# Where the key and query transposes and the sums stand among the slots of an attention stage on TensorE

## The chip, the cores and the metric

The kernel runs on one core of a Trainium2 chip. The metric is the device time of one execution in microseconds (us). PE is TensorE, the matrix engine; PEld is its loading of weights; DVE, ACT and POOL are the vector, scalar and general engines; SP issues most of the DMAs.

## What is computed

Attention over 8 batches, 12 heads, 448 tokens and a head size of 64, with normalized queries and keys, and then a mixture of experts over the 3584 tokens, each of which goes to one of 8 experts:

```python
q_n, k_n = rmsnorm(q, g_q), rmsnorm(k, g_k)
scores = (1 / sqrt(64)) * q_n @ k_n.transpose(0, 1, 3, 2)
attn = softmax(scores)                       # over the keys
x = (attn @ v) -> [3584, 768]                # tokens x (heads * 64)
logits = x @ w_gate + modality_bias[modality_id]
e = argmax(logits);  gate = softmax(logits)[e]
out = gate * (relu(x @ w1[e]) @ w2[e])       # for each token its expert
```

## The kernel before

The first half of the time is attention, the second the experts. The change touches attention alone.

A **unit** is two heads of one batch, so there are 48 units (`NU`). A unit has seven **slots** (`NJ`), one for each group of 128 rows out of its 2 x 448 = 896. Attention is a loop over slots `n`; slot `n` belongs to unit `i` and has the place `j` in it (`i, j = divmod(n, NJ)`, so `j` runs from 0 to 6). In each slot PE computes, in this order:

- `st` (L851): the scores of the current unit, keys by queries, two matmuls (four in place 3) into one buffer of the two-buffer PSUM pool `ps_s`. ACT takes the exponential of it into `p`.
- `sa` (L823, in place 3 L818): scores of a unit two ahead, only to find the maxima; DVE reduces them.
- then whatever else the slot has.

The other work of PE is spread over the slots by a table of numbers, `PLAN`. For a unit `u` an entry such as `'tk': 21` puts the work into slot `7u - 21`; others count from a later unit. The works, with their line on PE:

- `tr` (L752): four transposes of normalized keys (`tk`) or queries (`tq`), 112 rows each, into one buffer of the two-buffer PSUM pool `ps_t`. Four readers empty it, in this order: `a0`, the first copy on ACT (`xw<-tr`), whose result goes on by two DMAs on SP; the difference on DVE between the transposes and that copy (`xw<-tr,xw`), with two more DMAs; then two copies of half the rows on ACT, `a1` and `a2` (`w1w<-tr`). ACT's `a1` waits for DVE's difference.
- `mt` (L834): one transpose of the unit's maxima, also from `ps_t`. ACT copies it (`xw<-mt`) and a DMA takes it to the place where the scores read it.
- `av` (L890): value products, attention times values, in four parts `c` of two matmuls. They stand in places 1, 1, 4 and 6 (`'av': (1, 1, 4, 6)`).
- `sums` (L905): the sums of the exponentials, once for two units, in place 2 (`'sm': 2`); `gates` (L912): the gate logits, once for four units, in place 6.
- `recips` (`sp`, L924): transposes of sums and gate logits, once for four units, from `ps_t`; in place 2 (`'rc': 9`). DVE reads them.
- `xt` (L947): transposes of a unit's output, from `ps_t`, in place 4. DVE reads them.

Five kinds of work so share the two buffers of `ps_t`. A buffer is taken by whoever asks when it is free, and else the one whose last reader is done first.

The other engines' part is laid out by lists: what is put at `pre["A"]` or `pre["V"]` for slot `n` is done on ACT or DVE before that slot's exponential and maxima, what is put at `post` after them:

```python
run(pre["A"], n)
run(pre["V"], n)
pump(...)                 # one operation of the routing, if there is any
if ex:
    ex()                  # exponential of this slot's st, on ACT
for f in sm:
    f()                   # maxima of this slot's sa, on DVE
pump(...)
run(post, n)
```

ACT also squares queries and keys for the norms (`xrw<-r`) and DVE reduces the squares (`at_hlw<-xrw`); POOL multiplies by the norms. Each engine works its list in order, so an instruction that waits holds back all behind it.

Of the kernel before, what the change touches and what calls it, by code (L numbers as in the profile page):

```python
# [30 lines left out]
NT1 = NB1 * S  # L31
BIG = float(1 << 20)
ET = mybir.EngineType
PLAN = {'rtj': 6, 'rushat': 36, 'av': (1, 1, 4, 6), 'xt': 4, 'xte': (2, 5), 'sm': 2, 'la': 6, 'rc': 9, 'csv': (1,), 'csj': (3, 6), 'csd': (1, 1), 'cse': (2, 1), 'sa': 14, 'mt': 6, 'tk': 21, 'tq': 18, 'nq': 26, 'nk': 26, 'sk': 49, 'sq': 50, 'rs': 48, 'ld': 58, 'first': {('sq', 0): -22, ('sk', 0): -22, ('nk', 0): -21, ('nq', 0): -20, ('sq', 1): -21, ('sk', 1): -21, ('sq', 2): -20, ('sk', 2): -20, ('nk', 1): -18, ('nq', 1): -18, ('tk', 0): -18, ('tq', 0): -18, ('sa', 0): -14, ('tk', 1): -13, ('tq', 1): -11, ('sa', 1): -7, ('mt', 0): -6, ('tk', 2): -8, ('tq', 2): -8, ('nq', 2): -14, ('nk', 2): -14, ('nq', 3): -2, ('nk', 3): -1, ('sq', 3): -8, ('sk', 3): -8, ('sq', 4): -9, ('sk', 4): -9, ('sq', 6): -6, ('sk', 6): -4, ('sk', 7): -7, ('sq', 8): 5, ('sk', 8): 5, ('nk', 7): 15, ('nq', 9): 31, ('tq', 3): 4, ('mt', 1): 0, ('nq', 5): 10, ('mt', 8): 50, ('rs', 0): -21, ('rs', 2): -18, ('nq', 8): 35, ('rs', 5): -7, ('mt', 2): 8, ('nq', 7): 18, ('mt', 5): 30, ('sk', 9): 15, ('tk', 9): 43, ('mt', 6): 36, ('nq', 6): 13, ('sa', 5): 22, ('rs', 7): 0, ('rs', 8): 6, ('mt', 4): 22, ('nk', 4): 4, ('ld', 9): 6, ('tk', 5): 15}, 'rs0': {0: 0, 2: 1, 5: 0, 7: 0, 8: 2}, 'sastep': 1, 'start': -22, 'warm': {5: 2, -6: 16, -12: 4, -7: 2, -9: 4, -21: 4}, 'warmn': 2, 'early': 1, 'late0': 1, 'pmp0': 2, 'ramp': 10, 'pmp': (0, 0, 1, 1, 1, 0, 1), 'nv': [(2, 1)], 'pmpa': (1, 0, 1, 0, 1, 1, 1), 'rush': (1, 1, 1), 'ps': [(7, 1)], 'pa': [(6, 0), (6, 1), (5, 1), (5, 0)], 'rtr': 6, 'sml': 4}
MANUAL = {ET.PE, ET.DVE, ET.Activation, ET.Pool, ET.SP}
IOFF = bass.IndirectOffsetOnAxis

# [29 lines left out]
def kernel(  # L67
# [15 lines left out]
    V, A, G = (Deferred(e, n) for e, n in ((nc.vector, "op"), (nc.scalar, "act"), (nc.gpsimd, "dma")))  # L83
# [562 lines left out]
    if True:  # L646
# [33 lines left out]
        def sumsq(u, i):  # L680
# [4 lines left out]
            sq = sq_b[i]  # L685
            if (u, i) in PLAN["pa"]:
                x = T[u][nm].rearrange("p h c d -> p (h c) d")
# [143 lines left out]
        def mt(u):  # L831
            t = T[u]
            ps = ps_t.tile([128, 512], F32, tag="t", name=f"mt{u}")
            PE.transpose(ps[0:NJ, :128], t["mx"], idn)  # L834

            def act():
                ms = ms_b[u % 2]
                A.copy(ms, ps[0:NJ, :128])
                (A if u < 2 else SY).dma_start(t["ql"][64:65].rearrange("p h s -> p (h s)").bitcast(F32),
                            ms.bitcast(F32))  # L840

            return act
# [206 lines left out]
        P = PLAN  # L1049
# [6 lines left out]
        puts, done, routed = [], [], []  # L1056
# [32 lines left out]
        def warm(n):  # L1089
            for _ in range(n):  # L1090
                PE.matmul(wps[:, :128], lhsT=ones, rhs=idn, start=True, stop=True)
# [10 lines left out]
        pre = {e: {} for e in "AV"}  # L1102
        post, fin = {}, {}
        P = PLAN
        CSV, CSJ, CSD, CSE = (P[x] for x in ("csv", "csj", "csd", "cse"))

        def at(where, n, fn):
            where.setdefault(n, []).append(fn)
# [19 lines left out]
        P = PLAN  # L1128
# [39 lines left out]
        for n in range(P["start"], NJ * NU):  # L1168
            i, j = divmod(n, NJ)
            todo = {}  # L1170
            for what, *a in plan.get(n, ()):
                todo.setdefault(what, []).append(tuple(a))
            state["n"] = n
            state["rush"] = i >= P["rushat"]
            warm(P["warm"].get(n, 0))
            ex = st(i, j) if 0 <= i < NU else None
            sm = [sa(*a) for a in todo.get("sa", ())]
            if n < 0:
                warm(P["warmn"])
            for u, c in todo.get("av", ()):  # L1180
                av(u, c)
                if c == 3:
                    at(pre["A"] if j else post, n + (j > 0), lambda u=u: avcopy(u))
            for a in todo.get("sums", ()):
                sums(*a)
            for a in todo.get("gates", ()):
                at(pre["A"], n + 1, gates(*a))
            for a in todo.get("tr", ()):
                a0, a1, a2, d_ = tr(*a)
                if a[0] < P["early"]:  # L1190
                    at(pre["A"], n + 1, a1)
                    at(pre["A"], n + 1, a2)
                    at(pre["A"], n + P["late0"], a0)
                    at(pre["V"], n + P["late0"], d_)
                    continue
                at(pre["A"], n + 1, a0)
                at(pre["V"], n + 1, d_)
                at(post, n + 1, a1)
                at(pre["A"], n + 2, a2)
            for a in todo.get("mt", ()):  # L1200
                at(pre["A"], n + 1, mt(*a))
            for a in todo.get("recips", ()):
                at(pre["V"], n + 1, recips(*a))
                at(pre["V"], n + 1, lambda a=a: done.append(a[0]))
            for a in todo.get("xt", ()):
                at(pre["V"], n + 1, xt(*a))
            if puts and n >= puts[0][0] and n - lastput[0] >= 3:
                lastput[0] = n
                puts.pop(0)[1]()
            if i == NU - 1 and j in XRJ:  # L1210
                at(pre["V"], n + 1, xtr(0, X0, XRJ.index(j)))
            run(pre["A"], n)
            run(pre["V"], n)
            pump(P["rush"][0] if state["rush"] else P["pmpa"][j], j)
            if ex:
                ex()
            for f in sm:
                f()
            pump(P["rush"][1] if state["rush"] else P["pmp"][j], j)
            run(post, n)  # L1220
            for a in todo.get("sq", ()):
                at(pre["V"], n + 1, sumsq(*a))
            for a in todo.get("rs", ()):
                fast.append(("exp", lambda a=a: rstd(*a)))
            pump(P["rush"][2] if state["rush"] else P["pmp0"] if n < P["ramp"] else 0, j)
            if 0 <= i < NU and j in CSJ:
                h = CSJ.index(j)
                more, rest = csum(i, h)
                at(fin, n + CSD[h], more)
                at(fin, n + CSE[h], rest)  # L1230
            run(fin, n)
            for a in todo.get("norm", ()):
                while fast and (a[0] < 9 or a[0] % 3 == 0):
                    pump(1)
                norm(*a, V if a in P["nv"] else G)
                if a[0] == 0 and a[1] == 1:
                    gain_product()
            for a in todo.get("load", ()):
                load(*a)
            if done and len(routed) < B - 1 and done[-1] >= (NP * len(routed) + 5) // 4:  # L1240
                b = len(routed)
                routed.append(b)
                slow.append(("exp", lambda b=b: route(b)))
                slow.append(("pe", lambda b=b: at(pre["V"], state["n"] + 1, route_mm(b))))
                slow.append(("exp", lambda b=b: route_pos(b)))
                if b < B - 2:
                    slow.append(("exp", lambda b=b: put_all(b)))
                if b == NB1 - 1:
                    slow.append(("exp", tables1))
            if n == -4:  # L1250
                load_v(0)
                load_gate()
                SY.dma_start(l_d.rearrange("(p r) w -> p (r w)", p=128), zt)
            for h in range(2):
                if n == NJ * (NU - 5 + h) + 4:
                    wload(0, 0, (h,))
            if n == NJ * (NU - 3) + 4:
                X0 = xload(0)
            if i >= NU - 2 and j < 6:
                split1(i - NU + 2, j, j + 1)  # L1260
            if j < NJ - 1:
                continue
            if i == 0:
                slow += deferred(gate_consts)
            if i == NU - 1:
                for m in sorted(fin):
                    run(fin, m)
                wload(0, 1)
            if (i + 1) % 3 == 0 and 0 < (i + 1) // 3 < 2 * B:
                load_v((i + 1) // 3)  # L1270
# [121 lines left out]
    nv = nc.values_load(state["nsl"], min_val=0, max_val=NS1 + NS2)  # L1392
# [52 lines left out]
```

## Time and profile before

| what | value |
|---|---|
| three timed runs, median (lowest to highest) | 1141.43 us (1140.6 to 1145.1) |
| the profiled execution: time | 1139.65 us |
| the profiled execution: span from first to last instruction | 1137.9 us |
| its granted clock, mean | 0.98 |

The profile is of one execution. A group of its instructions is named by line, engine, operation and out<-in, by the program's names of its buffers: `tr`, `mt`, `sp`, `xt`, `st`, `sa`, `av`, `sm` are the PSUM tiles above. Many works share the line L52 on ACT, DVE and POOL, since a helper records them; they are told apart by their tiles. In the timeline the first column is the start, the second the duration. In a row of windows the busy time of PE, PEld, DVE, ACT and POOL follows, each with its count, then the granted clock of PE (1.00 is full speed), the DMA share and GB/s. In a row of waits stand the total in us, the number of waits and the longest.

### The profile page before, as it was taken

The page shows a single profiled execution, that of the slowest core. Times are in us where ns is not written, and L with a number is a line of the kernel's source. Part 1 is how long each engine was busy: PE and PEld are TensorE (multiplying, and loading weights), DVE is VectorE, ACT ScalarE, POOL GpSimd, SP SyncE. Part 2 cuts the span into 40 slices and gives each one's busy share as a digit, 9 for nine tenths or more (in the row PEclk, how much of TensorE's full clock was granted, in tenths as well). Part 3 has the DMA queues.
Part 4 walks back from the last instruction along what each step waited for, and adds up shares of the span by engine and source line. Part 5 has one row for each costly group of instructions (what it writes and reads, how often), then busy time and mean ns, then how long its engine had stood idle before and what let it go on. Part 6 is the DMA issues. An engine that isn't in the chain of part 4 may idle for free. (4 is left out here: it accounts for less than half of the span.)

```text
span 1137.9 us, 19896 instructions
## 1 busy us (share of the span) xinstructions
PE 1089.8 (96%) x6678; PEld 856.9 (75%) x6678; DVE 863.7 (76%) x1598; ACT 827.7 (73%) x1605; POOL 656.8 (58%) x665
## 2 busy tenths in 40 slices
PE   7899999999999999999999999999999999999993
PEld 6655655566565565555568899999999999999981
DVE  4676778988779988789688987767777677776770
ACT  6878888778787787775666677668776687766770
POOL 4577677777777787777764565444244433345430
PEclk8899999999999999999999999999999999999996
DMA  7656567666576666665725111111161111111360
GB/s 170 169 127 154 127 174 173 167 161 148 141 180 162 163 144 160 168 147 114 212 66 189 26 46 59 40 57 56 43 252 41 56 43 56 32 40 56 115 186 11
DMA packets 101345, 131.78 MB, mean 116 GB/s; under 512 B 29979, under 2 KB 95983, under 8 KB 99696
## 3 DMA queue, kind: packets, MB, share of 16 engines
q1 hardware_dynamic: 83588, 88.57, 32.0%
q0 software_dynamic: 17616, 41.80, 11.7%
q8 instruction: 57, 0.93, 0.4%
q14 instruction: 56, 0.46, 0.1%
q10 hardware_dynamic: 28, 0.01, 0.0%
HBM read 148.74 MB, written 22.38 MB: 150 GB/s over the span
## 5 line engine op out<-in xcount | busy, mean ns | idle before, releaser
L485 PE MATMUL ph<-xw,w1w 128*128 128x256 f32 x2016 | 246.1, 283 | 1.8 <-DVE hlw L52 1.0
L485 PEld LDWEIGHTS ph<-xw,w1w 128*128 128x128 f32 x2016 | 243.9, 192 | 3.8 <-issue 1.4
L52 DVE TENSOR_REDUCE at_hlw<-sa 128x1 f32<-128x448 f32 x336 | 206.9, 618 | 48.3 <-PE sa L823 30.0
L52 DVE TENSOR_TENSOR w1w<-r,w1w 128x256 fp32r<-128x256 f32 x360 | 221.0, 672 | 13.8 <-ACT w1w L52 13.5
L52 ACT CAST w1w<-r 128x256 fp32r<-128x256 f32 x360 | 224.8, 722 | 0.0
L851 PE MATMUL st<-w1w 128*128 128x448 f32 (+1 forms) x480 | 191.7, 448 | 1.1 <-ACT r2w L52 0.8
L851 PEld LDWEIGHTS st<-w1w 128*128 128x128 f32 (+1 forms) x480 | 107.3, 239 | 45.1 <-ACT r2w L52 21.2
L52 ACT ACTIVATE hhw<-ph 128x512 fp32r<-128x512 f32 x56 | 33.5, 598 | 121.8 <-PE ph L485 121.8
L52 POOL TENSOR_TENSOR r2w<-r2w 128x448 f32<-128x448 f32 (+1 forms) x72 | 82.4, 1144 | 68.4 <-DVE r2w L52 30.6
L52 ACT ACTIVATE r2w<-st 128x448 f32<-128x448 f32 x168 | 90.0, 541 | 40.7 <-PE st L851 35.7
L823 PE MATMUL sa<-w1w 128*128 128x448 f32 (+1 forms) x288 | 110.6, 385 | 8.9 <-DVE at_hlw L52 5.8
L515 PE MATMUL py<-w2lw,hhw 128*128 128x384 f32 x448 | 113.9, 335 | 0.0
L851 PE MATMUL st<-w1w,w2ha 65*128 65x448 f32 x288 | 102.5, 376 | 3.1 <-DMA r2w<-in_v_dram 2.5
L52 ACT ACTIVATE at_w2lw<-st 128x448 f32<-128x448 f32 x168 | 89.3, 540 | 13.4 <-PE st L851 11.6
L52 POOL TENSOR_TENSOR xrw<-r,at_hlw 112x512 f32<-112x512 f32 x95 | 97.4, 1045 | 2.5 <-PE tr L752 2.2
L52 POOL DMA_INDIRECT out_dram<-yw,lb_oi x22 | 28.3, 1286 | 122.0 <-ACT yw L52 118.9
L515 PEld LDWEIGHTS py<-w2lw,hhw 128*128 128x128 f32 x448 | 80.9, 188 | 0.0
L52 DVE SCALAR_TENSOR_TENSOR hlw<-ph,hhw 128x512 fp32r<-128x512 f32 x56 | 38.7, 691 | 51.9 <-ACT hhw L52 51.9
L52 ACT ACTIVATE w1w<-tr,gs 64x448 fp32r<-64x448 f32 x96 | 60.3, 629 | 23.0 <-DVE xw L52 22.3
L52 POOL TENSOR_TENSOR r2w<-r2w,at_w2lw 64x448 f32<-64x448 f32 (+1 forms) x48 | 54.9, 1144 | 38.0 <-DVE r2w L52 19.5
L851 PEld LDWEIGHTS st<-w1w,w2ha 65*128 65x128 f32 x288 | 70.9, 246 | 5.4 <-DMA r2w<-in_v_dram 2.7
L52 ACT ACTIVATE xrw<-r 112x512 f32<-112x512 f32 (+1 forms) x124 | 64.6, 526 | 9.7 <-DMA r<-in_k_dram 7.2
(297 smaller groups left out, 2297.9 us busy)
## 6 DMA issues: line engine op xcount, KB each, us to landing
w1w<-xw SPq DMA_DIRECT2D x312, 112.0 KB
r<-in_q_dram SPq DMA_DIRECT2D x48, 224.0 KB
r<-in_k_dram SPq DMA_DIRECT2D x48, 224.0 KB
w2ha<-xw SPq DMA_DIRECT2D x72, 112.0 KB
x_d<-at_w2hb SPq DMA_DIRECT2D x8, 672.0 KB
x_d<-yw SPq DMA_DIRECT2D x8, 672.0 KB
r2w<-in_v_dram SPq DMA_DIRECT2D x16, 288.0 KB
at_w2lw<-in_v_dram SPq DMA_DIRECT2D x16, 288.0 KB
```

The costliest lines, as they stand in the source:

```text
L52: return fn(*a, **kw)
L485: PE.matmul(ps[:, i], lhsT=lt_, rhs=rt_[:, c], start=n == 0, stop=n == 17)
L515: PE.matmul(ps[n][:, :384], lhsT=lt_[:, j, 128 * t : 128 * t + 128], rhs=rt_[:, 384 * n : 384 * n + 384], start=j == 0 and m == 0, stop=j ...
L823: PE.matmul(ps[:, :S], lhsT=t["qq"][r, h, a : a + 128], rhs=t["kk"][h][r], start=True, stop=True)
L851: PE.matmul(ps[:, :S], lhsT=l, rhs=t["qq"][:, h] if first else t["ql"][:, h], start=first and (j != 3 or h == 0), stop=not first and (j != ...
```

## The change

Numbers of the table, and the order within a slot. By the table `sm` goes from 2 to 4, `rc` from 9 to 8, `tk` from 21 to 20, `tq` from 18 to 17 (and one norm, of queries in unit 9, from slot 31 to 32, so that it stays behind what it needs):

```diff
-PLAN = {... 'sm': 2, 'la': 6, 'rc': 9, ... 'tk': 21, 'tq': 18, ...}
+PLAN = {... 'sm': 4, 'la': 6, 'rc': 8, ... 'tk': 20, 'tq': 17, ...}
```

So keys go from place 0 to 1, queries from 3 to 4, sums from 2 to 4 and recips from 2 to 1. Places 1, 4 and 6 hold value products. In the loop the transposes (`tr`, `mt`, `recips`, `xt`) are now issued ahead of the value products, sums and gates, and the readers of `tr` are put at other points of ACT's and DVE's lists:

```diff
+            for a in todo.get("tr", ()):
+                a0, a1, a2, d_ = tr(*a)
+                if a[0] < P["early"]:
+                    at(pre["A"], n + 1, a1)
+                    at(pre["A"], n + 1, a2)
+                    at(pre["A"], n + P["late0"], a0)
+                    at(pre["V"], n + P["late0"], d_)
+                    continue
+                at(post, n, a0)
+                at(post, n, d_)
+                at(pre["A"], n + 1, a1)
+                at(post, n + 1, a2)
+            for a in todo.get("mt", ()):
+                at(pre["A"], n + 1, mt(*a))
+            for a in todo.get("recips", ()):
+                at(pre["V"], n + 1, recips(*a))
+                at(pre["V"], n + 1, lambda a=a: done.append(a[0]))
+            for a in todo.get("xt", ()):
+                at(pre["V"], n + 1, xt(*a))
             for u, c in todo.get("av", ()):
                 av(u, c)
                 if c == 3:
...
                 sums(*a)
             for a in todo.get("gates", ()):
                 at(pre["A"], n + 1, gates(*a))
-            for a in todo.get("tr", ()):
-                a0, a1, a2, d_ = tr(*a)
...
-                at(pre["A"], n + 1, a0)
-                at(pre["V"], n + 1, d_)
-                at(post, n + 1, a1)
-                at(pre["A"], n + 2, a2)
-            for a in todo.get("mt", ()):
-                at(pre["A"], n + 1, mt(*a))
-            for a in todo.get("recips", ()):
-                at(pre["V"], n + 1, recips(*a))
-                at(pre["V"], n + 1, lambda a=a: done.append(a[0]))
-            for a in todo.get("xt", ()):
-                at(pre["V"], n + 1, xt(*a))
```

**PE, places 1 to 3 of unit 10**, a unit in which `recips` stand. Before (the number in a name after the tile is the tile's running number; `tr_1` are keys, `tr_0` queries; the keys' transposes of this unit stand just ahead of the first row, in place 0):

```order
L851 MATMUL st_1_1677<-w1w 128x448
L851 MATMUL st_1_1677<-w1w,w2ha 128x448
L823 MATMUL sa_1_1680<-w1w 128x448
L890 MATMUL av_1682<-at_w2lw 64x448 x4
L834 MATMUL mt_1687<-idn,at_hlw 7x128
L851 MATMUL st_2_1699<-w1w 128x448
L851 MATMUL st_2_1699<-w1w,w2ha 128x448
L823 MATMUL sa_2_1702<-w1w 128x448
L905 MATMUL sm_1704<-at_w2hb,sel 32x448 x2
L905 MATMUL sm_1704<-at_hhw,sel 32x448 x2
L924 MATMUL sp_1709<-idn,at_hlw 112x128 x4
L851 MATMUL st_3_1723<-w1w 128x448 x2
```

and now, in the same places:

```order
L851 MATMUL st_1_1672<-w1w 128x448
L851 MATMUL st_1_1672<-w1w,w2ha 128x448
L823 MATMUL sa_1_1675<-w1w 128x448
L752 MATMUL tr_1_1677<-idn,xrw 128x112 x4
L834 MATMUL mt_1682<-idn,at_hlw 7x128
L924 MATMUL sp_1684<-idn,at_hlw 112x128 x4
L890 MATMUL av_1689<-at_w2lw 64x448 x4
L851 MATMUL st_2_1703<-w1w 128x448
L851 MATMUL st_2_1703<-w1w,w2ha 128x448
L823 MATMUL sa_2_1706<-w1w 128x448
L851 MATMUL st_3_1724<-w1w 128x448 x2
```

The transposes of keys and of the sums and the value products are now one run between the scores of places 1 and 2, with the three users of `ps_t` first; the sums are gone from place 2 and stand in place 4, behind value products there. In units without `recips` the run is the same without `sp`.

**ACT in the same places** (with what each waits for; the number behind an engine's name means nothing here). Before:

```order
L52 ACTIVATE xw<-tr_1_1664,gs 128x448 [waits DMAHW1_49,DMAHW0_49,PE_49]
L52 ACTIVATE r2w<-st_1_1677 128x448 [waits PE_49]
L52 ACTIVATE w1w<-tr_1_1664,gs 64x448 [waits DVE_49]
L52 ACTIVATE w1w<-tr_1_1664,gs 64x448
L52 CAST xw<-mt_1687 7x128 [waits DMAHW4_49,PE_49]
L53 ACTIVATE at_hlw<-at_hlw,lnb 112x48 [waits DVE_49]
L52 ACTIVATE r2w<-st_2_1699 128x448 [waits PE_49,Pool_49]
```

and now:

```order
L52 ACTIVATE r2w<-st_1_1672 128x448 [waits PE_49]
L52 ACTIVATE xw<-tr_1_1677,gs 128x448 [waits DMAHW1_49,DMAHW0_49,PE_49]
L52 ACTIVATE w1w<-tr_1_1677,gs 64x448 [waits DVE_49]
L52 CAST xw<-mt_1682 7x128 [waits DMAHW4_49,PE_49]
L53 ACTIVATE at_hlw<-at_hlw,lnb 112x48
L52 ACTIVATE r2w<-st_2_1703 128x448 [waits PE_49,Pool_49]
L53 ACTIVATE at_hlw<-at_hlw,lnb 112x48 [waits Activation_49]
L52 ACTIVATE w1w<-tr_1_1677,gs 64x448
```

The first copy of the keys stands behind the exponential of place 1 instead of ahead of it, and the second half copy behind the exponential of place 2. On DVE (not shown) the reduction of the squares and the maxima of place 1 stood behind the keys' difference and now stand ahead of it.

More of the change, by code (lines that the diff above doesn't have):

```diff
@@ L33 @@
 ET = mybir.EngineType
-PLAN = {'rtj': 6, 'rushat': 36, 'av': (1, 1, 4, 6), 'xt': 4, 'xte': (2, 5), 'sm': 2, 'la': 6, 'rc': 9, 'csv': (1,), 'csj': (3, 6), 'csd': (1, 1), 'cse': (2, 1), 'sa': 14, 'mt': 6, 'tk': 21, 'tq': 18, 'nq': 26, 'nk': 26, 'sk': 49, 'sq': 50, 'rs': 48, 'ld': 58, 'first': {('sq', 0): -22, ('sk', 0): -22, ('nk', 0): -21, ('nq', 0): -20, ('sq', 1): -21, ('sk', 1): -21, ('sq', 2): -20, ('sk', 2): -20, ('nk', 1): -18, ('nq', 1): -18, ('tk', 0): -18, ('tq', 0): -18, ('sa', 0): -14, ('tk', 1): -13, ('tq', 1): -11, ('sa', 1): -7, ('mt', 0): -6, ('tk', 2): -8, ('tq', 2): -8, ('nq', 2): -14, ('nk', 2): -14, ('nq', 3): -2, ('nk', 3): -1, ('sq', 3): -8, ('sk', 3): -8, ('sq', 4): -9, ('sk', 4): -9, ('sq', 6): -6, ('sk', 6): -4, ('sk', 7): -7, ('sq', 8): 5, ('sk', 8): 5, ('nk', 7): 15, ('nq', 9): 31, ('tq', 3): 4, ('mt', 1): 0, ('nq', 5): 10, ('mt', 8): 50, ('rs', 0): -21, ('rs', 2): -18, ('nq', 8): 35, ('rs', 5): -7, ('mt', 2): 8, ('nq', 7): 18, ('mt', 5): 30, ('sk', 9): 15, ('tk', 9): 43, ('mt', 6): 36, ('nq', 6): 13, ('sa', 5): 22, ('rs', 7): 0, ('rs', 8): 6, ('mt', 4): 22, ('nk', 4): 4, ('ld', 9): 6, ('tk', 5): 15}, 'rs0': {0: 0, 2: 1, 5: 0, 7: 0, 8: 2}, 'sastep': 1, 'start': -22, 'warm': {5: 2, -6: 16, -12: 4, -7: 2, -9: 4, -21: 4}, 'warmn': 2, 'early': 1, 'late0': 1, 'pmp0': 2, 'ramp': 10, 'pmp': (0, 0, 1, 1, 1, 0, 1), 'nv': [(2, 1)], 'pmpa': (1, 0, 1, 0, 1, 1, 1), 'rush': (1, 1, 1), 'ps': [(7, 1)], 'pa': [(6, 0), (6, 1), (5, 1), (5, 0)], 'rtr': 6, 'sml': 4}
@@ new lines @@
+PLAN = {'rtj': 6, 'rushat': 36, 'av': (1, 1, 4, 6), 'xt': 4, 'xte': (2, 5), 'sm': 4, 'la': 6, 'rc': 8, 'csv': (1,), 'csj': (3, 6), 'csd': (1, 1), 'cse': (2, 1), 'sa': 14, 'mt': 6, 'tk': 20, 'tq': 17, 'nq': 26, 'nk': 26, 'sk': 49, 'sq': 50, 'rs': 48, 'ld': 58, 'first': {('sq', 0): -22, ('sk', 0): -22, ('nk', 0): -21, ('nq', 0): -20, ('sq', 1): -21, ('sk', 1): -21, ('sq', 2): -20, ('sk', 2): -20, ('nk', 1): -18, ('nq', 1): -18, ('tk', 0): -18, ('tq', 0): -18, ('sa', 0): -14, ('tk', 1): -13, ('tq', 1): -11, ('sa', 1): -7, ('mt', 0): -6, ('tk', 2): -8, ('tq', 2): -8, ('nq', 2): -14, ('nk', 2): -14, ('nq', 3): -2, ('nk', 3): -1, ('sq', 3): -8, ('sk', 3): -8, ('sq', 4): -9, ('sk', 4): -9, ('sq', 6): -6, ('sk', 6): -4, ('sk', 7): -7, ('sq', 8): 5, ('sk', 8): 5, ('nk', 7): 15, ('nq', 9): 32, ('tq', 3): 4, ('mt', 1): 0, ('nq', 5): 10, ('mt', 8): 50, ('rs', 0): -21, ('rs', 2): -18, ('nq', 8): 35, ('rs', 5): -7, ('mt', 2): 8, ('nq', 7): 18, ('mt', 5): 30, ('sk', 9): 15, ('tk', 9): 43, ('mt', 6): 36, ('nq', 6): 13, ('sa', 5): 22, ('rs', 7): 0, ('rs', 8): 6, ('mt', 4): 22, ('nk', 4): 4, ('ld', 9): 6, ('tk', 5): 15}, 'rs0': {0: 0, 2: 1, 5: 0, 7: 0, 8: 2}, 'sastep': 1, 'start': -22, 'warm': {5: 2, -6: 16, -12: 4, -7: 2, -9: 4, -21: 4}, 'warmn': 2, 'early': 1, 'late0': 1, 'pmp0': 2, 'ramp': 10, 'pmp': (0, 0, 1, 1, 1, 0, 1), 'nv': [(2, 1)], 'pmpa': (1, 0, 1, 0, 1, 1, 1), 'rush': (1, 1, 1), 'ps': [(7, 1)], 'pa': [(6, 0), (6, 1), (5, 1), (5, 0)], 'rtr': 6, 'sml': 4}
@@ L1187 @@
                 at(pre["A"], n + 1, gates(*a))
-            for a in todo.get("tr", ()):
-                a0, a1, a2, d_ = tr(*a)
[L1190 to L1195, printed above, removed]
-                at(pre["A"], n + 1, a0)
-                at(pre["V"], n + 1, d_)
-                at(post, n + 1, a1)
-                at(pre["A"], n + 2, a2)
-            for a in todo.get("mt", ()):
-                at(pre["A"], n + 1, mt(*a))
-            for a in todo.get("recips", ()):
-                at(pre["V"], n + 1, recips(*a))
-                at(pre["V"], n + 1, lambda a=a: done.append(a[0]))
-            for a in todo.get("xt", ()):
-                at(pre["V"], n + 1, xt(*a))
             if puts and n >= puts[0][0] and n - lastput[0] >= 3:
```

## The prediction

> **What bounds the kernel now.** I read the page's head and slices first, then a window of the attention stage, then the waits of PE, and last the order of time on PE.
>
> ```profile
> span 1137.9 us, 19896 instructions
> PE 1089.8 (96%) x6678; PEld 856.9 (75%) x6678; DVE 863.7 (76%) x1598; ACT 827.7 (73%) x1605; POOL 656.8 (58%) x665
> PEclk8899999999999999999999999999999999999996
> 160.00:220.00 60.00, 60.00 (x318) 37.25 (x318) 52.27 (x106) 48.35 (x107) 42.26 (x46) 1.00 0.65 162
> ```
>
> The last row is a window of attention (us, then busy time of PE, PEld, DVE, ACT, POOL, the granted clock, the DMA share). PE is busy all 60 us, DVE 52 and ACT 48. So PE sets the pace there, and DVE and ACT have some room, but little. The waits of PE over the whole run agree; the rows give the total in us, how often, and the longest:
>
> ```profile
> PE sa L823 <- DVE at_hlw L52: 5.8, 8, 1.5
> PE sa L823 <- DMA w1w<-xw: 2.6, 4, 1.1
> PE sp L924 <- ACT w1w L52: 0.5, 1, 0.5
> ```
>
> PE hardly ever waits, so time goes away only if PE needs less of it, and comes back one for one if PE is made to wait. Where PE's own time goes is seen in the starts of its groups; here is a unit (first column the start, second the duration, whose end is modelled; I use differences of starts):
>
> ```profile
> 279.89 0.37 PE L823 MATMUL sa<-w1w 128*128 128x448 f32 x1
> 280.10 0.55 PE L752 MATMUL tr<-idn,xrw 112*128 112x112 f32 x4
> 280.42 0.52 PE L851 MATMUL st<-w1w 128*128 128x448 f32 x1
> 280.77 0.37 PE L851 MATMUL st<-w1w,w2ha 65*128 65x448 f32 x1
> 280.98 0.37 PE L823 MATMUL sa<-w1w 128*128 128x448 f32 x1
> 281.28 1.72 PE L890 MATMUL av<-r2w 128*64 128x448 f32 x8
> 282.94 0.28 PE L834 MATMUL mt<-idn,at_hlw 128*7 128x128 f32 x1
> 282.97 0.52 PE L851 MATMUL st<-w1w 128*128 128x448 f32 x1
> 283.32 0.37 PE L851 MATMUL st<-w1w,w2ha 65*128 65x448 f32 x1
> ...
> 288.01 0.37 PE L851 MATMUL st<-w1w 128*128 128x448 f32 x1
> 288.21 0.36 PE L851 MATMUL st<-w1w,w2ha 65*128 65x448 f32 x1
> 288.42 0.37 PE L823 MATMUL sa<-w1w 128*128 128x448 f32 x1
> ```
>
> In a plain slot a matmul follows the last by 0.20 or 0.21 (288.01, 288.21, 288.42). After a group of transposes the first score matmul takes 0.35 (280.42 to 280.77), and after the value products with the maxima's transpose it takes 0.35 too (282.97 to 283.32). So each return from these groups to the score matmuls costs 0.14. Going into the value products costs about 0.09: they start 0.30 after `sa` (280.98 to 281.28), transposes only 0.21 after it (279.89 to 280.10).
>
> **What the change saves.** A key or query transpose that shared its slot with no value product now shares one, so one return of 0.14 per moved transpose is gone. What the new passage from transposes to value products costs, no row shows; it is between nothing and the 0.09 of the passage from `sa` to `av`, and at best the 0.09 now paid there is saved as well. That is 0.05 to 0.23 a slot; I take 0.15, near the return alone, since that part surely goes. Key and query follow the plan's general rule in 43 and 44 of 48 units, so 87 slots x 0.15 = 13 us (4 to 20).
>
> The sums come from a slot of their own:
>
> ```profile
> 297.91 0.37 PE L823 MATMUL sa<-w1w 128*128 128x448 f32 x1
> 298.21 0.57 PE L905 MATMUL sm<-at_w2hb,sel 128*32 128x448 f32 x2
> 298.61 0.55 PE L905 MATMUL sm<-at_w2hb,sel 128*32 128x448 f32 x2
> 299.10 0.65 PE L924 MATMUL sp<-idn,at_hlw 128*112 128x128 f32 x4
> ```
>
> They too pay 0.30 instead of 0.21 to get in, and a return; behind value products both go, 0.09 + 0.14, about 0.2 (0.05 to 0.23 by the same bounds). 18 pairs of units x 0.2 = 4 us (1 to 4). The saving together is **17 us (5 to 24)**.
>
> **What it adds: a wait of PE for a PSUM buffer.** The transposes use a pool of two buffers. In every fourth unit up to unit 36 the transposes of the sums (`sp`, the recips) move from slot 2 to slot 1, right behind the keys' transpose and that of the maxima (`mt`). That makes three users of two buffers in one slot, with no score matmul between them. `sp` can only take the buffer of `mt`: the keys' buffer is last read by a copy that ACT does after the exponential of the next slot, whose matmuls stand behind `sp` on PE. And the copy of `mt` stands in ACT behind the keys' first copy and its second copy, and the second waits for DVE's difference. That chain is in the trace of before, in a unit with `sp`, in another order:
>
> ```profile
> 246.62 0.55 PE L752 MATMUL tr<-idn,xrw 112*128 112x112 f32 x4
> ...
> 247.63 0.63 ACT L52 ACTIVATE xw<-tr,gs 128x448 fp32r<-128x448 f32 x1
> 248.15 0.54 ACT L52 ACTIVATE r2w<-st 128x448 f32<-128x448 f32 x1
> 248.29 0.68 DVE L52 SCALAR_TENSOR_TENSOR xw<-tr,gs,xw 128x448 fp32r<-128x448 f32 x1 [0.82 <-ACT xw L52]
> 248.90 0.68 DVE L52 TENSOR_REDUCE at_hlw<-xrw 112x8 f32<-112x512 f32 x1
> 249.01 1.27 ACT L52 ACTIVATE w1w<-tr,gs 64x448 fp32r<-64x448 f32 x2 [0.32 <-DVE xw L52]
> ...
> 250.31 0.26 ACT L52 CAST xw<-mt 7x128 fp32r<-7x128 f32 x1
> ```
>
> Counted from the start of the transposes, the chain is at least 0.55 (transposes) + 0.63 (first copy) + 0.68 (difference) + 0.63 (one of the two half copies) + 0.26 (copy of `mt`) + four hand-overs of 0.04 (248.29 + 0.68 to 249.01) = 2.9 us. PE itself would be ready for `sp` after the transposes' 0.32 and some 0.05 for `mt`, about 0.4. So PE waits at least 2.5 us. Both engines may come late on top. DVE now does the reduction of the squares (248.90, 0.68) and that of this slot's scores ahead of the difference; on ACT the exponential stands ahead of the first copy. Worked forward from these rows: the score matmuls come first, so the transposes start at 246.62 + 3 x 0.206 = 247.24 and PE is ready for `sp` at 247.6; the exponential runs from 247.63, the first copy from 248.1 to 248.75; DVE does the squares and the scores (0.68 + 0.61) from about 247.75 to 249.0 and the difference to 249.7; half copy and `mt`'s copy end at 250.6. That is 3.0 us. I take 2.9 (2.5 to 3.1): 9 units x 2.9 = **26 us (22 to 28)**. The value products are queued behind `sp` and could have filled it, but PE works in order. Nothing hides this wait: PE is the engine that bounds. Before, the slot of `sums` and a whole slot of scores lay between, and `sp` waited 0.5 once, by the row above.
>
> **What a wait does to the clock.** Five stretches and what followed:
>
> ```profile
> 289.40:292.80 3.40, 2.27 (x13) 0.79 (x11) 1.24 (x3) 2.49 (x5) 1.00 (x2) 1.00 0.59 116
> 292.80:296.20 3.40, 3.40 (x12) 2.18 (x14) 2.02 (x4) 1.84 (x4) 2.42 (x3) 0.50 0.58 157
> 381.50:384.90 3.40, 2.15 (x9) 0.95 (x8) 3.40 (x7) 1.75 (x6) 2.73 (x3) 1.00 0.25 57
> 384.90:388.30 3.40, 3.40 (x26) 2.23 (x26) 2.37 (x6) 3.18 (x8) 2.21 (x2) 1.00 0.92 242
> 518.10:521.50 3.40, 1.83 (x8) 1.03 (x8) 3.33 (x6) 2.23 (x6) 3.24 (x4) 1.00 0.46 101
> 521.50:524.90 3.40, 3.40 (x13) 0.50 (x12) 3.33 (x8) 0.14 (x1) 2.69 (x4) 0.50 0.17 36
> ```
>
> A stretch of 3.40 us with 1.13 idle (3.40 - 2.27) was followed by one at clock 0.50, one with 1.57 idle too, one with 1.25 idle was not. A stretch at half clock in which PE is busy throughout loses 1.7 us. A wait of 2.9 lies in one stretch or is cut in two, and then the larger part is at least 1.45. So I expect it to cost the clock about eight times in ten: 9 x 1.7 x 0.8 = **12 us (0 to 15)**. The Trainium skill, "TensorE: Matmul & The Clock Gate", section "HAM oscillation — how this bites in real kernels", says that only gaps of PE above about 3.4 us cost the clock; by that rule this term is nothing, and the sum 12 us less. The trace speaks against it, with half clock after waits of 1.1 and 1.5.
>
> **The rest.** The keys' and queries' copies come half a slot later on ACT and DVE, and their DMAs on SP's queue with them, in the order they had. In plain units too, the exponential of slot 2 now ends behind the chain worked out above, at about 250.6 + 0.54 = 251.1 in that unit's time, and the scores of slot 4, which need its buffer, come 3.95 after the transposes' start (0.4, then value products 1.7, slot 2 with its return 0.8, and slot 3 with five matmuls 1.05), at 251.2. That just fits; where DVE is held up by routing it does not, and PE waits some tenths. On the other side the long waits let DVE and ACT catch up, and some of the 5.8 + 2.6 us above may go. I take **3 us (-4 to +12)**. `mt` and the transposes of the outputs change places with value products in slots they had already: nothing, since the return is paid once either way. The MoE stage and the last units are as before.
>
> **Sum.** The profiled execution took 1139.65 us, its span 1137.9; the three timed runs have their median at 1141.43 (1140.6 to 1145.1), so I let the profiled time stand. 1139.65 - 17 + 26 + 12 + 3 = 1163.7, that is **1164 us**.
>
> **The rivals.**
> - *The waits are there, the clock holds* (what the skill's rule would give; here, waits shorter than a stretch that the clock lets pass, as it did at 381.50). 1139.65 - 17 + 26 + 3 = 1152, between 1143 and 1158. Against it: the stretches at 289.40 and 518.10. Chance 0.20.
> - *Faster: the merged slots are worth it.* The place is `sp` in slot 1; its wait would have to stay under 17 / 9 = 1.9 us for the change to break even. If it were 0.5, as once before, with the clock held, and the saving at 20: 1139.65 - 20 + 9 x 0.5 = 1124. For it: PE's time does shrink in every unit. Against: the chain of durations alone is 2.9 us. Chance 0.08.
> - *Slower still: ordinary units wait as well.* DVE is at 52 of 60 us, and a difference that comes 1 us later in the units with routing makes slot 4 wait for the exponential of slot 2. With 12 units of 1 us and the clock lost in half of them (6 x 0.5 x 3.4 = 10), and the other terms as forecast: 1163.7 - 3 + 22 = 1183. For it: no slack in the sum above. Against: each such wait drains the delay. Chance 0.12.
> - *The saving isn't there*, when the passage from transposes to value products costs what the return did: then the 13 us are gone and the rest gives 1177, at the upper end of the forecast's case.
>
> **How the numbers follow.** The forecast (wait and clock) has 0.60 and lies between 1149 and 1176, by a saving of 10 to 24, waits of 22 to 28 and a clock term of 8 to 15. For 8 in 10 the range goes from 1145 to 1178: it leaves out the faster case (0.08), a little of the clock-holds case (0.03) and most of the last (0.08). A measurement of this kernel can tell about 0.5%, 5.7 us, from no change. Faster by more than that needs the second rival: 0.08. Within it lie the low end of the first rival and the ground between: 0.12. Slower: 0.80.
>
> **What would show it.** Right: nine waits of PE at `sp` for ACT of 2.5 to 3.1 us each, some 26 us together; more slices of PEclk under full speed between 100 and 500 us, with stretches at 0.50 behind these waits; plain units shorter by 0.3 to 0.4 us, with transposes followed by value products and one return per slot. Wrong: `sp` waits under 1.9 us; or the clock stays at 1.00 behind them; or units without `sp` are not shorter; or PE's waits lie at `st` of slot 4.

## The result, and the profile after

| kernel | median (lowest to highest) | ratio to before, 95% interval |
|---|---|---|
| before | 1143.26 us (1140.6 to 1146.49) | 1 |
| changed | 1184.52 us (1182.01 to 1187.12) | 1.036 (1.0317 to 1.0402) |

The row of before has one run more than the three shown above. The change costs 41 us, where the forecast had 24 and its range ended at 1178. The sign was right and the size was not. The profiled execution of the changed kernel took 1186.55 us. The head of its page and the granted clock in 40 slices:

```profile
span 1184.8 us, 19838 instructions
PE 1105.8 (93%) x6678; PEld 873.1 (74%) x6678; DVE 857.8 (72%) x1598; ACT 814.9 (69%) x1605; POOL 657.3 (55%) x665
PEclk8899999999899998999999999999999999999997
```

PE is busy 93% of a longer span instead of 96%, with 16 us more of busy time for the same 6678 matmuls. Two slices more are below 9 tenths of the clock, both in attention. The waits of PE (total in us, how often, the longest) say what it waited for:

```profile
PE sp L924 <- ACT xw L52: 24.3, 9, 3.8
PE st L851 <- ACT at_w2lw L52: 6.0, 8, 2.6
...
PE st L851 <- ACT r2w L52: 4.1, 6, 1.4
```

Nine waits at `sp` for ACT, 24.3 us: the wait that the prediction had priced at 26. The waits of `st` for ACT, 10.1 us, are large now. One of the nine, on all engines (start, duration, and in brackets the idle time ahead with what ended it):

```profile
112.17 0.28 PE L834 MATMUL mt<-idn,at_hlw 128*7 128x128 f32 x1
112.30 0.55 ACT L52 ACTIVATE r2w<-st 128x448 f32<-128x448 f32 x1
...
112.73 0.65 ACT L52 ACTIVATE xw<-tr,gs 128x448 fp32r<-128x448 f32 x1
113.06 0.61 DVE L52 TENSOR_REDUCE at_hlw<-sa 128x1 f32<-128x448 f32 x1
...
113.59 0.68 DVE L52 SCALAR_TENSOR_TENSOR xw<-tr,gs,xw 128x448 fp32r<-128x448 f32 x1
...
114.30 0.63 ACT L52 ACTIVATE w1w<-tr,gs 64x448 fp32r<-64x448 f32 x1 [0.92 <-DVE xw L52]
...
114.83 0.24 ACT L52 CAST xw<-mt 7x128 fp32r<-7x128 f32 x1
...
115.12 0.65 PE L924 MATMUL sp<-idn,at_hlw 128*112 128x128 f32 x4 [2.67 <-ACT xw L52]
...
115.70 2.90 PE L890 MATMUL av<-at_w2lw 128*64 128x448 f32 x8
```

This is the chain of the prediction, link by link: exponential, first copy, DVE's reduction of this slot's maxima (the one of the squares stands ahead of it, left out here), its difference, the half copy, the copy of `mt`, and only then `sp`. PE is idle for 2.67 us ahead of 115.12, with the value products queued behind `sp`. They then take 2.90 instead of 1.72, because the clock is at half. The windows around this wait and around the one at 366 (us, busy time of PE, PEld, DVE, ACT, POOL, clock, DMA share, GB/s) show both outcomes:

```profile
112.70:116.10 3.40, 0.98 (x6) 0.60 (x8) 1.82 (x5) 1.45 (x4) 2.82 (x3) 1.00 0.95 258
116.10:119.50 3.40, 3.40 (x11) 1.38 (x8) 0.90 (x5) 0.00 (x0) 0.00 (x0) 0.50 0.27 63
...
363.00:366.40 3.40, 0.91 (x7) 0.55 (x6) 2.26 (x4) 2.47 (x6) 3.40 (x4) 1.00 0.32 84
366.40:369.80 3.40, 3.36 (x17) 1.97 (x18) 1.37 (x8) 0.28 (x1) 0.65 (x1) 1.00 0.49 109
```

Half clock stands beside or behind eight of the nine waits, and this one at 366 has none. In two of the eight it begins only 0.7 and 0.8 us into the wait at `sp` (at 314.1 and 464.3), just behind another wait of PE, of 1.53 and 1.46 us; what started it in these two is not shown. Now a plain unit, where the saving should have been; the first rows are from the place of slots 2 and 4, which experiment e5 needs:

```profile
281.18 0.52 ACT L52 ACTIVATE at_w2lw<-st 128x448 f32<-128x448 f32 x1
281.38 0.36 PE L818 MATMUL sa<-xw,w2ha 128*128 128x448 f32 x1
281.75 0.74 PE L851 MATMUL st<-w1w 128*128 128x448 f32 x2
...
287.34 0.37 PE L823 MATMUL sa<-w1w 128*128 128x448 f32 x1
...
287.75 0.37 PE L851 MATMUL st<-w1w,w2ha 65*128 65x448 f32 x1
287.96 0.37 PE L823 MATMUL sa<-w1w 128*128 128x448 f32 x1
288.16 0.55 PE L752 MATMUL tr<-idn,xrw 112*128 112x112 f32 x4
288.55 0.28 PE L834 MATMUL mt<-idn,at_hlw 128*7 128x128 f32 x1
288.75 1.72 PE L890 MATMUL av<-at_w2lw,r2w 128*64 128x448 f32 x8
290.40 0.54 PE L851 MATMUL st<-w1w 128*128 128x448 f32 x1
290.78 0.37 PE L851 MATMUL st<-w1w,w2ha 65*128 65x448 f32 x1
```

Measure the work of two slots, each from its `sa` to the second score matmul behind it. Now: 287.34 to 287.75 is 0.41 for the slot without transposes, 287.96 to 290.78 is 2.82 for the merged one, together 3.23. Before, by the prediction's rows: 279.89 to 280.77 is 0.88 for the transposes' slot, 280.98 to 283.32 is 2.34 for that of the value products, together 3.22. **The merged slots save nothing.** Piece by piece: one return is gone (-0.14) and the value products' entry from `sa` (0.30) became that of the transposes (0.20: -0.10). But `mt` follows the keys' transposes after 0.39, where a score matmul followed after 0.32 (+0.07); the value products follow `mt` after 0.20, where a score matmul followed it after 0.03 (+0.17); and the return from value products alone is 0.38 instead of 0.35 (+0.03). The five sum to +0.03, and with roundings of 0.01 in the rest to +0.01. This unit is no exception. Over the slots of the stage in which PE does not wait (100 to 580 us) the medians for the keys are 0.875 + 2.339 before and 0.409 + 2.824 now, +0.02; for the queries, in slots without sums, 0.875 + 1.955 before and 0.409 + 2.401 now, -0.02.

From the starts of `mt`, 47 distances between neighbouring units can be worked out in each kernel. The nine units with `sp` in the merged slot are longer by 38.3 us together (2.5 to 5.3 each), all the others by 5.0. Behind the last `mt` the two profiled executions differ by another 4.8 us (562.3 before, 567.1 now); e8 below, with the same work there, takes 563.3, so most of that varies from execution to execution.

### The profile page after: what moved, and what is told of

Read it like the earlier page. It is cut to its first block, busy times and chain, and to the rows that moved or that the text cites. A ratio compares the mean times of both kernels' runs of the same rounds, so it can differ in the third digit from the quotient of the medians.

```text
span 1184.8 us, 19838 instructions
## 1 busy us (share of the span) xinstructions
PE 1105.8 (93%) x6678; PEld 873.1 (74%) x6678; DVE 857.8 (72%) x1598; ACT 814.9 (69%) x1605; POOL 657.3 (55%) x665
## 5 line engine op out<-in xcount | busy, mean ns | idle before, releaser
L851 PEld LDWEIGHTS st<-w1w 128*128 128x128 f32 (+1 forms) x480 | 109.7, 241 | 125.7 <-ACT xw L52 35.9
L851 PE MATMUL st<-w1w 128*128 128x448 f32 (+1 forms) x480 | 186.2, 438 | 11.2 <-ACT at_w2lw L52 6.0
L52 DVE TENSOR_REDUCE at_hlw<-xrw 112x8 f32<-112x512 f32 x91 | 61.6, 682 | 33.5 <-ACT xrw L52 32.9
L52 ACT CAST w1w<-tr 64x448 fp32r<-64x448 f32 x96 | 50.5, 526 | 48.0 <-DVE xw L52 43.4
```

Of the source, the lines that this page charges most:

```text
L52: return fn(*a, **kw)
L851: PE.matmul(ps[:, :S], lhsT=l, rhs=t["qq"][:, h] if first else t["ql"][:, h], start=first and (j != 3 or h == 0), stop=not first and (j != ...
```

## The experiments

The theory after the result: the waits at `sp` and their clock cost what was forecast, the merged slots save nothing because the passage from transposes to value products is dear, and some tenths in the other units come from the new order of the readers on ACT. The main rival: the merged slots do save their 17 us, and the waits and the clock cost more than forecast.

**e1: no wait.** In the nine units `sp` takes its buffer from another PSUM pool; everything else is as changed.

```diff
         def recips(g):
-            ps = ps_t.tile([128, 512], F32, tag="t", name=f"sp{g}")
+            pool, tag = (ps_m, "m") if g < 9 else (ps_t, "t")
+            ps = pool.tile([128, 512], F32, tag=tag, name=f"sp{g}")
```

> The changed kernel, but the transposes of the sums take their PSUM buffer from the pool of the sums and gate logits, which is free at that point, so that they need not wait for ACT's copy of the maxima. Theory (the nine waits and the clock behind them are the whole loss, 38 us, and the merged slots save nothing because the passage from transposes to value products costs PE 0.20 us, as much as what it replaces): waits of PE at sp under 1 us in all, and 1146 us (1141 to 1150) beside 1143 for the kernel before. Rival (the forecast's saving of 17 us is there, and each wait costs some 6 us in all instead of 4): 1126 us (1121 to 1131).

Measured: 1152.75 us (1149.29 to 1155.95), ratio 1.0065 (1.0041 to 1.0089). The first two waits of PE, and the one that e5 needs:

```profile
PE st L851 <- ACT at_w2lw L52: 5.8, 7, 2.6
PE st L851 <- ACT r2w L52: 4.7, 9, 1.5
...
PE sa L823 <- DVE at_hlw L52: 3.4, 4, 1.4
```

No row names `sp` any more. The rival falls: with the waits gone the kernel is still slower than before, so they hid no saving of 17 us. The time is some 7 us above the theory's and outside its range, and `st` still waits 10.5 us for ACT.

**e2: the wait behind the value products.** `recips` are issued after the value products of the slot.

```diff
-            for a in todo.get("recips", ()):
-                ...
             for a in todo.get("xt", ()):
...
                 at(pre["A"], n + 1, gates(*a))
+            for a in todo.get("recips", ()):
+                ...
```

> The changed kernel, but in the slot the transposes of the sums stand behind the value products, with the same wait for ACT. The value products (1.65 us) then cover most of the wait. Theory: PE waits about 1.0 us at each of nine sp instead of 2.7, the clock mostly holds (none or two stretches at half clock behind them), so 1146 + 9 + 2 = 1157 us (1150 to 1162). Rival (saving of 17 there, each wait dear): with the waits cut to two fifths, 1126 + 9 x 2.5 = 1149 us. If the clock goes down after waits of 1.0 too, 1165.

Measured: 1159.83 us (1156.38 to 1164.77), ratio 1.0113 (1.0058 to 1.0168).

```profile
PE sp L924 <- ACT xw L52: 8.9, 7, 2.1
```

Seven waits of 0.9 to 2.1 us are left, and no half clock stands behind any of them. So the value products fill part of the wait, and most of the cost came from where `sp` stood in the slot.

**e3: the sums alone.** The kernel before, with the sums in place 4.

```diff
-PLAN = {... 'sm': 2, ...}
+PLAN = {... 'sm': 4, ...}
```

> The kernel before with one number changed: the sums go from place 2 to place 4, behind value products and ahead of the outputs' transposes; no transposes of keys or queries move. Theory: sums and value products follow each other without a passage, so 0.3 us less for each of 18 pairs of units, 5 us: 1138 us (1135 to 1141). Rival (no merging saves anything): 1143 us.

Measured: 1138.54 us (1132.15 to 1143.42), ratio 0.9932 (0.9899 to 0.9966): **faster than both kernels**. Most units with sums and no `sp` are shorter by 0.15 to 0.22, which is the prediction's 0.2. Those with `sp`, which stays behind in place 2 and there still pays for its own return, are shorter by 0.15 at most. The interval (3.9 to 11.6 us) holds the forecast's 4 us at its lower end. This part of the change is good, and it is the one part with no transposes in it.

**e4: the order in the slot alone.** The kernel before, with `mt` and `xt` issued ahead of the value products of their slots; keys, queries and sums stay.

```diff
+            for a in todo.get("mt", ()):
+                at(pre["A"], n + 1, mt(*a))
+            for a in todo.get("xt", ()):
+                at(pre["V"], n + 1, xt(*a))
             for u, c in todo.get("av", ()):
...
-            for a in todo.get("mt", ()):
-                ...
-            for a in todo.get("xt", ()):
-                ...
```

> The kernel before, with only the order inside two slots changed: the transposes of the maxima (place 1) and of the outputs (place 4) stand ahead of the value products instead of behind them. Nothing else moves. Theory (the passage from transposes to value products costs 0.20 where the other order pays 0.03 on leaving the transposes): 0.10 us more for each of two slots in some 45 units, 9 us: 1152 us (1148 to 1155). Rival (the order in the slot is free, as the forecast had it): 1143 us (1141 to 1146).

Measured: 1149.8 us (1144.39 to 1152.18), ratio 1.0036 (1.001 to 1.0063), that is 4 us (1 to 7), between the rival's nothing and the theory's 9. PE in a unit:

```profile
283.34 0.37 PE L823 MATMUL sa<-w1w 128*128 128x448 f32 x1
283.55 0.27 PE L834 MATMUL mt<-idn,at_hlw 128*7 128x128 f32 x1
283.75 1.72 PE L890 MATMUL av<-r2w 128*64 128x448 f32 x8
...
285.79 0.37 PE L851 MATMUL st<-w1w,w2ha 65*128 65x448 f32 x1
...
288.11 0.37 PE L823 MATMUL sa<-w1w 128*128 128x448 f32 x1
...
290.13 0.37 PE L851 MATMUL st<-w1w,w2ha 65*128 65x448 f32 x1
```

The slot of `mt` takes 2.45 (283.34 to 285.79), where it took 2.34 with `mt` behind the value products. That of `xt` takes 2.02 (288.11 to 290.13). In e6, which keeps the old order of that slot, it takes 1.95 (rows below, 284.49 to 286.44). So to put transposes ahead of value products costs 0.11 and 0.07, together 0.18 a unit: the same matmuls, another order. The medians over all such slots, from this run and from before, give 0.11 and 0.06. Behind value products a transpose starts no later than scores do (1.66 after their start, 281.28 to 282.94 in the prediction's rows, against 1.65, 288.75 to 290.40 above), and a score matmul follows `mt` after 0.03 (282.94 to 282.97 in the prediction's rows); ahead of them `mt` hands over only after 0.20 (283.55 to 283.75).

**e5: the old order of the readers.** e1, with the readers of `tr` in their old lists on ACT and DVE (counted from the new slot).

```diff
-                at(post, n, a0)
-                at(post, n, d_)
-                at(pre["A"], n + 1, a1)
-                at(post, n + 1, a2)
+                at(pre["A"], n + 1, a0)
+                at(pre["V"], n + 1, d_)
+                at(post, n + 1, a1)
+                at(pre["A"], n + 2, a2)
```

> The kernel of e1 (changed kernel, other buffer for the transposes of the sums), with the readers of the key and query transposes put back where the kernel before had them in the lists of ACT and DVE (first copy and difference at the head of the next slot, half copies one and two points later). PE's order is that of e1. Theory (the rest of the loss in e1, 8 us, is the score matmuls waiting for ACT, 10.5 us in e1, because the exponential of place 2 now ends behind the keys' chain): waits of st for ACT fall under 4 us and the time to 1145 us (1141 to 1149). Rival (the rest is PE's own passages): it stays at 1152.

Measured: 1147.27 us (1141.43 to 1151.34), ratio 1.0024 (0.9998 to 1.0049). Its waits of PE:

```profile
PE sa L823 <- DVE at_hlw L52: 8.3, 8, 1.9
...
PE st L851 <- ACT r2w L52: 1.0, 1, 1.0
...
PE st L851 <- ACT at_w2lw L52: 0.6, 1, 0.6
```

The waits of `st` for ACT fall from 10.5 to 1.6 us and those of `sa` for DVE rise from 3.4 to 8.3; in sum the ratio falls by 0.004, about 5 us (1 to 9). The theory had 1145 (1141 to 1149). With neither the waits at `sp` nor ACT's new order in it, the kernel is still no faster than before, so ACT's order hid no saving either. This is the wait that the prediction said "just fits": in the changed kernel's rows above the first scores of slot 4 come 0.37 after the last `sa` (281.38 to 281.75) instead of 0.21, since ACT's exponential of slot 2, which ends at 281.70 (281.18 + 0.52), holds their buffer.

**e6 and e7: the transposes behind the value products.** e6 is the kernel before with the sums in place 4, the keys in place 1 but, by the old order, behind the value products there, and `sp` in place 2 with e1's buffer. e7 moves the queries to place 4 in the same way.

```diff
-PLAN = {... 'sm': 2, ... 'tk': 21, 'tq': 18, ...}
+PLAN = {... 'sm': 4, ... 'tk': 20, 'tq': 18, ...}     # e6
+PLAN = {... 'sm': 4, ... 'tk': 20, 'tq': 17, ...}     # e7
```

> The kernel before with the sums in place 4 as in e3, and the keys' transposes moved to place 1 but behind the value products instead of ahead of them; the transposes of the sums stay in place 2 and take the other buffer. Queries stay. Theory (leaving transposes for scores is paid once instead of twice, and no passage from transposes to value products is made: 0.07 us a slot): 43 x 0.07 = 3 us on top of e3's 6: 1135 us (1131 to 1138). Rival (it is the value products, not the order, that matter): as e3, 1138.5, or slower by waits for ACT.

> As e6, and the queries' transposes too, to place 4 behind value products and sums. Theory: another 3 us by the passages, 1132 us, unless the queries' DMAs land late: the transposes end some 1.7 us nearer to the first matmul that reads them. Then waits of sa for DMA over 5 us and 1136 to 1145.

Measured: e6 1152.04 us (1148.79 to 1157.26), ratio 1.0069 (1.0039 to 1.0098); e7 1167.01 us (1164.35 to 1168.9), ratio 1.019 (1.0143 to 1.0237). Both times were missed; for e7 the late DMAs had been named as a risk, but with a time of 1145 at most. e6 on PE:

```profile
279.41 0.37 PE L823 MATMUL sa<-w1w 128*128 128x448 f32 x1
...
281.37 0.60 PE L752 MATMUL tr<-idn,xrw 112*128 112x112 f32 x4
281.81 0.28 PE L834 MATMUL mt<-idn,at_hlw 128*7 128x128 f32 x1
...
282.19 0.37 PE L851 MATMUL st<-w1w,w2ha 65*128 65x448 f32 x1
...
284.49 0.37 PE L823 MATMUL sa<-w1w 128*128 128x448 f32 x1
...
286.44 0.37 PE L851 MATMUL st<-w1w,w2ha 65*128 65x448 f32 x1
```

279.41 to 282.19 is 2.78, and with the plain slot's 0.41 the two take 3.19, against 3.22 before. Merging in the better order so saves 0.03 for the keys, not 0.14: the return that goes away is paid for by the transposes themselves, which take 0.44 between value products and `mt` (281.37 to 281.81) instead of 0.32 ahead of scores. In both runs PE waits for other work instead:

```profile
PE sa L823 <- DMA w1w<-xw: 12.7, 7, 6.3
PE sa L823 <- DVE at_hlw L52: 9.7, 14, 2.7
```

These are e7's first waits: `sa` waits 12.7 us for DMAs of transposed rows, where it waits 3.6 us in e6, so some 9 us come with the queries, which now stand a slot later and behind the value products. Half of the 12.7 is a single wait of 6.3. In e6 about 9 us go in units 40 to 43, with half clock in three stretches; what starts that was not tried apart.

**e8 and e10: the wait filled.** The changed kernel, with matmuls of constants ahead of `sp` in the nine units: nine in e8, four in e10. `sp` still starts when ACT is done, so only the idle time, and with it the clock, can change.

```diff
+            if todo.get("recips") and n < 7 * 42:
+                wt = ps_m.tile([128, 512], F32, tag="m", name=f"fill{n}")
+                for _ in range(9):
+                    PE.matmul(wt[:, :128], lhsT=ones, rhs=idn, start=True, stop=True)
             for a in todo.get("recips", ()):
```

> The changed kernel with nine matmuls of constants (2.1 us, their result is read by nobody) put ahead of the transposes of the sums in each of the nine slots, so that PE works through most of its wait for ACT. Theory (a wait costs its length, and about 0.8 us more on average by the clock): no half clock behind these slots, the wait itself as long as before, 1153 + 24 = 1177 us (1172 to 1180). Rival (the clock costs nothing there): 1184 us as before, or more.

> The changed kernel with four matmuls of constants, about 1.0 us, ahead of sp in the nine units, so that PE idles some 1.2 us less there and waits about 1.7 us (0.9 to 3.0) instead of 2.7; nothing is left out. The time of the wait itself does not change, so only the clock can. If the clock falls behind a wait of about 1.1 us in a stretch, as before's rows read, the half clock stays behind most of the nine and the time is 1181 to 1186. If the limit lies at about 2 us, as the runs with waits of 0.5 to 1.8 us and up to 2.1 us without half clock suggest, most of it goes and the time is 1174 to 1179.

Measured: e8 1175.73 us (1172.18 to 1177.74), ratio 1.0258 (1.0209 to 1.0308); e10 1182.61 us (1180.16 to 1187.35), ratio 1.036 (1.032 to 1.0401). One place in e8:

```profile
160.22 0.28 PE L834 MATMUL mt<-idn,at_hlw 128*7 128x128 f32 x1
160.34 2.17 PE L1197 MATMUL fill<-idn,ones 128*128 128x128 f32 x18
163.04 0.65 PE L924 MATMUL sp<-idn,at_hlw 128*112 128x128 f32 x4 [0.53 <-ACT xw L52]
163.62 1.72 PE L890 MATMUL av<-at_w2lw 128*64 128x448 f32 x8
```

`sp` is no earlier (2.82 after `mt`; in the same unit of the changed kernel 2.81, 161.46 to 164.27), but the value products run at full clock, and no half clock stands behind any of the nine. The nine units are then longer than before by 25.1 us instead of 38.3: the clock's price is 13 us there. By the ratios of the two kernels it is 12 us (0.0102), and the wait itself is 22 us (0.0193, from e1 to e8), each give or take some 7. In e10 the trace shows half clock behind one wait, of 1.78 us, and none behind six of 1.65 or one of 2.89. The wait of 1.78 and one of the six:

```profile
113.70:117.10 3.40, 1.62 (x15) 1.36 (x13) 2.08 (x4) 2.43 (x6) 3.40 (x4) 1.00 0.94 273
118.00:121.40 3.40, 3.40 (x10) 1.22 (x7) 0.97 (x5) 0.00 (x0) 0.00 (x0) 0.50 0.28 61
363.90:367.30 3.40, 1.76 (x15) 1.49 (x14) 2.22 (x4) 2.43 (x6) 3.40 (x4) 1.00 0.42 114
367.30:370.70 3.40, 3.40 (x17) 2.01 (x18) 1.42 (x8) 0.33 (x1) 0.62 (x1) 1.00 0.47 103
```

So in its profiled execution the clock was mostly spared at `sp`, as the second of its two cases had it, yet the time stayed near the changed kernel's. That execution lost some 4 us at 237 us, where half clock followed a wait that the trace puts down to nothing, and the other three executions were no faster. e10 therefore does not settle how short a wait must be; in e8 all nine waits, filled to about 0.5 (1.77 at most), kept the clock.

**e9: `sp` in its old place.** The changed kernel with `'rc': 9`, which puts `sp` in place 2, behind the scores there.

> The changed kernel with the transposes of the sums (recips) left in place 2, behind that place's scores, as before; all else as changed. Theory (the cost is the place right behind two other users of the pool): the value products and the scores of place 2, 1.65 + 0.38 + 0.41 us, now lie between the copy's chain of 2.9 us and sp, so sp waits 0.5 us or less in each of the nine units, no half clock stands behind it, and the time is that of the run in which sp had another buffer, about 1152 (1147 to 1158). Rival (the two buffers are short for three users wherever sp stands in the unit): sp waits 1 to 2 us in each of the nine units and the time is 1162 to 1172.

Measured: 1152.71 us (1150.56 to 1153.65), ratio 1.009 (1.0054 to 1.0126), where e1 has 1152.75.

```profile
PE sp L924 <- ACT xw L52: 1.9, 2, 1.2
```

Two short waits instead of nine: two buffers were enough for three users here when some 2.4 us of other work lay between. One number of the table, 9 turned to 8, cost some 30 us of the 41.

## Why the prediction was wrong, by its own steps

- **The wait at `sp`: right.** 26 us (22 to 28) forecast; 24.3 in the rows, 22 by the ratios of e1 and e8. The chain of durations, worked forward from another order, gave 3.0 us and the range's lower end 2.5; seven of the nine waited 2.5 to 3.0.
- **The clock: right.** 12 us forecast, 13 in the nine units, 12 by the ratios. "About eight times in ten" was eight of nine, but the sum is near in part by luck: two of the eight places had 6.8 us at half clock, which at 1.7 for each 3.4 makes 17, less where PE was idle in them, and two began just behind another wait. The Trainium skill, "TensorE: Matmul & The Clock Gate", section "HAM oscillation — how this bites in real kernels", would have had one at most: it sets the limit at idle gaps above about 3.4 us, and only one of the nine was longer (3.8). The measurement decides against it here.
- **The saving: wrong, and this is the step that failed.** The prediction put "the new passage from transposes to value products" at "between nothing and 0.09" and took 0.15 us a slot as saved. The passage takes 0.20, where a transpose handed over to scores in 0.03 and the return behind it cost 0.14; so it costs what the return did, and the 13 us were not there. The prediction had this as a rival ("when the passage from transposes to value products costs what the return did"), but gave it no chance of its own and left the slot's other transposes out of it.
- **"`mt` and the transposes of the outputs change places with value products in slots they had already: nothing": wrong, by the same passage.** The rows of e4 show 0.18 a unit, 8.6 us over 48 units, and its time a smaller 4 (1 to 7). Taken in this order, the keys' and queries' merging then does save about 0.09 a slot (for the keys 3.23 against 0.88 + 2.45 = 3.33; by the medians 0.09 for keys and 0.08 for queries), some 7 us, and by the rows the two cancel. A reader of before could have seen half of it: `mt` stood behind the value products there, and a score matmul 0.03 behind `mt`.
- **The sums: right.** 4 us forecast, 3.9 to 11.6 measured; e3 confirms the 0.2 in units without `sp`, and less in those with it.
- **The rest: 3 us (-4 to +12), in range.** ACT's order cost about 5 us (e1 against e5), where "just fits" was named as the risk.

In terms of the sum: instead of -17 + 26 + 12 + 3 = +24 the runs give about -4 (sums) + 0 (merging and order) + 22 to 24 (waits) + 12 to 13 (clock) + 5 (ACT) = +35 to +38, of 41 measured. The remaining 3 to 6 are within the intervals of these ratios, some 5 us each, and stay unassigned. By the ratios alone, from before by e3, e5, e1 and e8 to the changed kernel, the steps are -8, +10, +5, +22 and +12. The second, the merging with its order, is 10 us (6 to 15) there and 0 by the rows of slots without a wait. PE's waits explain part of it: `sa` waits 8.3 us for DVE in e5 and 4.4 in e3. The rest is open.

## What to carry to other kernels

In this kernel a matmul's cost on a busy PE belongs to the pair of neighbours: before moving one, list every passage that goes and every one that comes, also for work that only changes its order within a slot, and look each up as a difference of starts; a passage that no row shows deserves bounds as wide as the return that it replaces. Work that takes a buffer from a small pool wants other work between it and the users ahead, and behind such a wait the clock can take more: here half as much again (12 to 13 us on 22 to 24). Of a change with several parts, time the parts apart: here the sums alone made the kernel 0.7% faster (0.3 to 1.0%), inside a change that made it 3.6% slower.

## What had not been expected of the hardware

The order of the same matmuls matters by itself: transposes ahead of value products cost 0.07 to 0.11 us a slot more than behind them (e4), since value products start 0.20 behind `mt` and 0.30 behind `sa`, while scores start 0.03 behind `mt`. And the clock's answer to an idle PE has no fixed length in these runs: waits of 2.54 us (the changed kernel at 366), of 2.89 and, six times, of 1.65 us (e10) kept full clock, and one of 1.78 (e10) and the 1.13 idle ahead of 292.80 in before did not.
